# A 1x1 depthwise-separable convolution: halved weight loads with per-slice waits, dummy matmuls ahead of the data, PSUM emptied by ScalarE alone, and last stores split by partitions

## The chip, the cores and the metric

The kernel runs on one core of a Trainium2 chip. The metric is the device time of one execution in microseconds (us). The comparison quantity is the median over several executions. A separate, profiled execution gives the profile; its times are counted from the first instruction of its span.

The core has five engines that run their own instruction queues: TensorE (matmuls, "PE", with its weight loads "PEld"), VectorE ("DVE"), ScalarE ("ACT"), GpSimd ("POOL") and SyncE ("SP", here only a queue of DMA issues). They wait for one another through semaphores. ScalarE can issue DMAs too. SBUF is the working memory of 128 partitions; PSUM holds the results of matmuls in 8 banks.

## The reference

The input `x` is an image of 384 x 384 pixels with 384 channels, in bf16. The depthwise kernel `dw` has size 1 x 1, so the depthwise step multiplies each channel by one number, and the pointwise step is a matrix product with `pw` (384 x 384):

```
B, H, W, C = x.shape                       # 1, 384, 384, 384
out = xp * dw[0, 0][None, None, None, :]   # k = 1: no padding
return jnp.einsum('bhwc,cd->bhwd', out, pw)
```

So out[n, d] = sum over c of x[n, c] * dw[c] * pw[c, d], for 147,456 pixels n. Both `x` and the output are 113.2 MB.

## The kernel before, in words

**Tiling.** The pixels are cut into 288 supertiles of 512 pixels. Supertiles are grouped into 42 chunks, which are the units of loads and stores: 1, 1, 2, 4, then 34 chunks of 8, then 4, 2, 1, 1. A chunk of 8 supertiles is 3 MB. There are three input buffers `X` and three output buffers `O`, used in turn by chunk (t mod 3), two buffers `T` of transposed data and two sets `PS` of four PSUM banks, used in turn by supertile (s = even or odd).

**Weights.** `pw_r` receives four copies of `pw`, one for each group q of 32 partitions; it has six slices b with two halves r (or par) each. Each copy is one DMA (`load_pw`, L89), two of them issued by ScalarE and two by SP. `dwsel` gets the numbers `dw` from a small load `dwt` by four VectorE copies (L186). VectorE makes six of the twelve scaled slices `w_r` (L197) and ScalarE the other six (L199). The first of each waits until all four loads have landed (`s_pw` at 64).

**A supertile.** VectorE transposes it from `X` to `T` in two instructions, h = 0 and 1 (L174), each for three slices b; pairs of bf16 numbers are moved as one 32-bit word. TensorE then runs 6 x 2 x 4 = 48 matmuls (L134): slice b, half par, row group q. The four q use different 32-row strips of the array and different PSUM banks, so they run side by side; the 12 steps over (b, par) accumulate. The matmuls stand in a hardware loop of 144 iterations, two supertiles in each. Ahead of the loop TensorE waits for all twelve slices `w_r`. Within it, it waits for each half of `T`, and at the first step for the PSUM banks to be empty: for ScalarE (`s_a`) at q = 0 and for VectorE (`s_d`) at q = 3.

**Emptying PSUM.** When a supertile's matmuls are done, ScalarE copies the banks of q = 0 to 2 to `O` (L215, 128 x 1152 elements), and VectorE the bank of q = 3 (L212, 128 x 384). VectorE's queue alternates: the copy of supertile jj, then the two transposes of supertile jj + 2. A transpose waits until TensorE has read the old content of that half of `T`. At the first supertile of a chunk both wait until the store that used this `O` buffer three chunks ago has landed (`s_o`).

**Loads and stores.** SP issues everything in a fixed order: `load_x(0)`, the weights, `load_x(1)`, `load_x(2)`, and then for each chunk t `load_x(t + 3)` (L95) and `store(t)` (L107). `load_x(t + 3)` waits until chunk t has been transposed, and `store(t)` until chunk t's last copies are done. As the queue is in order, a load behind a waiting store waits too. At the end SP waits for all stores.

Of the kernel before, what the change touches and what calls it, by code (L numbers as in the profile page):

```python
# [7 lines left out]
BF16 = mybir.dt.bfloat16  # L8
F32 = mybir.dt.float32
U32 = mybir.dt.uint32  # L10
COPY = mybir.ActivationFunctionType.Copy
# [3 lines left out]
NO = 3  # L15
# [11 lines left out]
def kernel(  # L27
# [11 lines left out]
    nc = tc.nc  # L39
    P = nc.NUM_PARTITIONS  # L40
    B, H, W, C = x.shape
    assert dw.shape[0] == 1 and dw.shape[1] == 1, "only k=1 depthwise supported"
    D = pw.shape[1]
    N = B * H * W
    assert C == 384 and D == 384 and N % 1024 == 0
    NB = C // 64

    xf = x.rearrange("b h w c -> (b h w) c")
    of = out.rearrange("b h w d -> (b h w) d")

    NS = N // 512
    chunks = _chunks(NS)
    NT = len(chunks)
    s0 = [sum(chunks[:t]) for t in range(NT)]

    consts = ctx.enter_context(tc.tile_pool(name="consts", bufs=1))
# [3 lines left out]
    pw_r = consts.tile([P, NB, 2, D], BF16, name="pw_r")  # L60
    w_r = consts.tile([P, NB, 2, D], BF16, name="w_r")
    dwt = consts.tile([32, NB, 2], BF16, name="dwt")
    dwsel = consts.tile([P, NB * 2], F32, name="dwsel")
    warm = consts.tile([P, 3], F32, name="warm")
    seed = consts.tile([P, 2], F32, name="seed")

    Xs = [bufp.tile([P, 4 * LMAX, C], BF16, name=f"X{i}") for i in range(NX)]
    Ts = [bufp.tile([P, NB, 256], BF16, name=f"T{i}") for i in range(2)]
    Os = [bufp.tile([P, 4 * LMAX * D], BF16, name=f"O{i}") for i in range(NO)]
    PS = [psum.tile([P, 4, 512], F32, name=f"ps{s}") for s in range(2)]  # L70
# [2 lines left out]
    s_t = [[nc.alloc_semaphore(f"s_t{i}{h}") for h in range(2)] for i in range(2)]  # L73
    s_pe = nc.alloc_semaphore("s_pe")
    s_a = [nc.alloc_semaphore(f"s_a{i}") for i in range(2)]
    s_d = [nc.alloc_semaphore(f"s_d{i}") for i in range(2)]
    s_o = [nc.alloc_semaphore(f"s_o{i}") for i in range(NO)]
    s_dw = nc.alloc_semaphore("s_dw")
    s_pw = nc.alloc_semaphore("s_pw")
    s_ds = nc.alloc_semaphore("s_ds")  # L80
    s_wr = nc.alloc_semaphore("s_wr")
    s_seed = nc.alloc_semaphore("s_seed")

    with tc.tile_critical():  # L84
        pw_v = pw.rearrange("(b w r) d -> w b (r d)", w=32, r=2)
        dw_v = dw.rearrange("a e (b w r) -> w (a e b) r", w=32, r=2)

        def load_pw(eng, q):
            eng.dma_start(pw_r[32 * q : 32 * q + 32].rearrange("w b r d -> w b (r d)"), pw_v).then_inc(s_pw, 16)  # L89

        def load_x(t):
            L = chunks[t]
            r = 512 * s0[t]
            src = xf[r : r + 512 * L, :].rearrange("(p s) c -> p (s c)", p=P)
            d = nc.sync.dma_start(Xs[t % NX][:, : 4 * L, :].rearrange("p s c -> p (s c)"), src)  # L95
            if t >= NX:
                je = s0[t - NX] + chunks[t - NX] - 1
                d._wait_ge(s_t[je % 2][1], je // 2 + 1)
            d.then_inc(s_x[t % NX], 16)

        def store(t):
            L = chunks[t]
            r = 512 * s0[t]
            je = s0[t] + L - 1
            nc.sync.wait_ge(s_d[je % 2], je // 2 + 2)
            dst = of[r : r + 512 * L, :].rearrange("(q p j) d -> p q (j d)", q=4, p=P)
            d = nc.sync.dma_start(dst, Os[t % NO][:, : 4 * L * D].rearrange("p (q e) -> p q e", q=4))  # L107
            d._wait_ge(s_a[je % 2], je // 2 + 2)
            d.then_inc(s_o[t % NO], 16)


        nc.scalar.dma_start(dwt[:], dw_v).then_inc(s_dw, 16)
        load_x(0)
        load_pw(nc.scalar, 2)
        load_pw(nc.sync, 0)
        load_pw(nc.scalar, 3)
        load_pw(nc.sync, 1)
        for t in range(1, NX):
            load_x(t)
        for t in range(NT):  # L120
            if t + NX < NT:
                load_x(t + NX)
            store(t)
        for o in range(NO):
            nc.sync.wait_ge(s_o[o], 16 * len(range(o, NT, NO)))


        def supertile(s, rv):
            for b in range(NB):
                for par in range(2):  # L130
                    for q in range(4):
                        if par == 0 and q == 0 and b in (0, 3):
                            nc.tensor.wait_ge(s_t[s][b // 3], rv)
                        mm = nc.tensor.matmul(  # L134
                            PS[s][:, q, :D],
                            lhsT=Ts[s][32 * q : 32 * q + 32, b, par::2],
                            rhs=w_r[32 * q : 32 * q + 32, b, par, :],
                            start=(b == 0 and par == 0),
                            stop=(b == NB - 1 and par == 1),
                            tile_position=(32 * q, 0),  # L140
                        )
                        if b == 0 and par == 0 and q == 0:
                            mm._wait_ge(s_a[s], rv)
                        elif b == 0 and par == 0 and q == 3:
                            mm._wait_ge(s_d[s], rv)
                        if b in (2, 5) and par == 1 and q == 3:
                            mm.then_inc(s_pe)

        nc.tensor.wait_ge(s_wr, 2 * NB)
        with nc.tensor.Fori(0, NS // 2, 1) as it:  # L150
            rv = nc.tensor.to_reg(it + 1)
            for s in range(2):
                supertile(s, rv)


        for s in range(2):
            nc.vector.memset(seed[:, s : s + 1], 0.0).then_inc(s_d[s])  # L157
        nc.gpsimd.memset(warm[:], 0.0).then_inc(s_seed)  # L158
        for s in range(2):
            c = nc.scalar.copy(warm[:, s + 1 : s + 2], warm[:, 0:1])  # L160
            if s == 0:
                c._wait_ge(s_seed, 1)
            c.then_inc(s_a[s])

        def transposes(t, j):
            jj = s0[t] + j
            L = chunks[t]
            s = jj % 2
            Xw = Xs[t % NX][:].bitcast(U32)[:, : 4 * L, :].rearrange("p (k l) c -> p k l c", l=L)
            Tw = Ts[s][:].bitcast(U32).rearrange("p b (i k) -> p b k i", k=4)  # L170
            for h in range(2):
                if h == 0 and j == 0:
                    nc.vector.wait_ge(s_x[t % NX], 16 * (t // NX + 1))  # L173
                ins = nc.vector.transpose(  # L174
                    out=Tw[:, 3 * h : 3 * h + 3],
                    in_=Xw[:, :, j, 96 * h : 96 * h + 96].rearrange("p k (b w) -> p b k w", w=32),
                )
                if jj >= 2:
                    ins._wait_ge(s_pe, 2 * (jj - 2) + h + 1)
                ins.then_inc(s_t[s][h])  # L180

        order = [(t, j) for t in range(NT) for j in range(chunks[t])]

        nc.vector.wait_ge(s_dw, 16)
        for q in range(4):
            nc.vector.tensor_copy(  # L186
                dwsel[32 * q : 32 * q + 32, :], dwt[:].rearrange("w b r -> w (b r)")
            ).then_inc(s_ds)
        transposes(*order[0])
        for b in range(NB):  # L190
            for r in range(2):
                eng = nc.vector if r == 0 else nc.scalar
                if b == 0:
                    eng.wait_ge(s_pw, 64)  # L194
                sc = dwsel[:, 2 * b + r : 2 * b + r + 1]
                if r == 0:
                    i = nc.vector.tensor_scalar_mul(w_r[:, b, r, :], pw_r[:, b, r, :], sc)  # L197
                else:
                    i = nc.scalar.activation(w_r[:, b, r, :], pw_r[:, b, r, :], COPY, scale=sc)  # L199
                if b == 0:  # L200
                    i._wait_ge(s_ds, 4)
                i.then_inc(s_wr)
        transposes(*order[1])

        for jj, (t, j) in enumerate(order):
            L = chunks[t]
            s = jj % 2
            Ov = Os[t % NO][:, : 4 * L * D].rearrange("p (q j d) -> p q j d", q=4, d=D)
            if j == 0 and t >= NO:
                nc.vector.wait_ge(s_o[t % NO], 16 * (t // NO))  # L210
                nc.scalar.wait_ge(s_o[t % NO], 16 * (t // NO))  # L211
            e = nc.vector.tensor_copy(Ov[:, 3, j, :], PS[s][:, 3, :D])  # L212
            e._wait_ge(s_pe, 2 * jj + 2)
            e.then_inc(s_d[s])
            a = nc.scalar.copy(Ov[:, 0:3, j, :], PS[s][:, 0:3, :D])  # L215
            a._wait_ge(s_pe, 2 * jj + 2)
            a.then_inc(s_a[s])
            if jj + 2 < NS:
                transposes(*order[jj + 2])


# [28 lines left out]
```

## Time and profile before

| what | value |
|---|---|
| median of 7 executions | 586.64 us (585.72 to 587.04) |
| profiled execution, its own time | 585.4 us |
| profiled execution, span from first to last instruction | 583.6 us |
| mean granted TensorE clock | 0.996 |
| TensorE matmuls busy | 563.5 us (97%), 13,824 instructions |
| VectorE busy | 563.9 us (97%) |
| ScalarE busy | 326.8 us (56%) |
| data moved by the DMA | 227.79 MB, mean 390 GB/s over the span |
| chain that ended last | PE 93%, DMA 5%, ACT 1% |

An engine's busy time is the time in which at least one of its instructions runs, so overlapping matmuls count once. The chain that ended last is followed back from the last instruction, at each step to what released it; what has a large share there sets the time. A group of instructions is one line of the kernel on one engine; "idle before" is the time in which the engine stood still just ahead of such an instruction. Lines such as L134 are line numbers of the kernel above.

### The profile page before, as it was taken

To read this page: it belongs to the slowest core of one execution; us is meant where nothing else is said; L and a number is where in the kernel's file an instruction comes from. 1 tells how busy PE (TensorE), PEld (TensorE's weight loads), DVE (VectorE), ACT (ScalarE), POOL (GpSimd) and SP (SyncE) were. 2 spreads that over 40 slices of the span, in tenths; PEclk is the share of its full clock that TensorE was granted. 3 is DMA by queue.
4 is the path that set the end of the run, shared out by engine and by line. 5 is a ranking of instruction groups with operands and counts; after the bars stand their busy time and mean duration, and the time that the engine had idled before them with its cause. 6 is when DMAs were issued, how large, how long until landed. Compare 5 with 4: busy or idle time off the path is not lost.

```text
span 583.6 us, 29852 instructions
## 1 busy us (share of the span) xinstructions
PE 563.5 (97%) x13824; PEld 412.9 (71%) x13824; DVE 563.9 (97%) x876; ACT 326.8 (56%) x297; POOL 0.3 (0%) x5
## 2 busy tenths in 40 slices
PE   1999999999999999999999999999999999999995
PEld 0667777777777777777777777777777777777773
DVE  3899999999999999999999999999999999999995
ACT  3555555555555555555656565555555555555553
POOL 0000000000000000000000000000000000000000
PEclk9999999999999999999999999999999999999998
DMA  8699999999999999999999999999999999999858
GB/s 295 247 429 421 426 424 425 418 386 403 418 388 400 416 389 390 415 387 417 408 392 415 395 409 418 389 409 402 400 409 400 390 401 419 393 394 419 324 222 312
DMA packets 29277, 227.79 MB, mean 390 GB/s; under 512 B 1616, under 2 KB 5456, under 8 KB 24656
## 3 DMA queue, kind: packets, MB, share of 16 engines
q1 hardware_dynamic: 28640, 227.09, 97.1%
q10 hardware_dynamic: 624, 0.59, 0.4%
q14 instruction: 12, 0.10, 0.0%
q8 instruction: 1, 0.02, 0.0%
HBM read 114.43 MB, written 113.25 MB: 390 GB/s over the span
## 4 chain that ended last, share of the span: by engine, by line
PE 93%; DMA 5%; ACT 1%; SPq 0%; issue 0%; DVE 0%; ACTq 0%; DVEq 0%
PE ps L134 93%; DMA X<-in_x_dram 2%; DMA out_dram<-O 1%; DMA pw_r<-in_pw_dram 1%; ACT O L215 1%; ACT w_r L199 1%; DVE T L174 0%; SPq L89 0%; SPq L107 0%; SPq L95 0%; SPq L245 0%; DVEq L173 0%; ACTq L211 0%; ACTq L194 0%; SPq L84 0%
## 5 line engine op out<-in xcount | busy, mean ns | idle before, releaser
L134 PE MATMUL ps<-w_r,T 32*128 32x384 bf16 x13824 | 563.5, 322 | 13.8 <-ACT w_r L199 13.0
L134 PEld LDWEIGHTS ps<-w_r,T 32*128 32x128 bf16 x13824 | 412.9, 93 | 164.0 <-issue 14.3
L215 ACT CAST O<-ps 128x1152 bf16<-128x1152 f32 x288 | 322.1, 1118 | 244.7 <-PE ps L134 242.9
L174 DVE STREAM_TRANSPOSE T<-X 128x384 uint32<-128x384 uint32 x576 | 449.8, 857 | 1.3 <-DMA X<-in_x_dram 1.2
L212 DVE CAST O<-ps 128x384 bf16<-128x384 f32 x288 | 160.4, 557 | 6.5 <-PE ps L134 4.3
L199 ACT ACTIVATE w_r<-pw_r,dwsel 128x384 bf16<-128x384 bf16 x6 | 3.1, 602 | 5.6 <-DMA pw_r<-in_pw_dram 5.6
L186 DVE CAST dwsel<-dwt 32x12 f32<-32x12 bf16 x4 | 0.7, 164 | 3.7 <-DMA dwt<-in_dw_dram 3.6
L197 DVE TENSOR_SCALAR w_r<-pw_r,dwsel 128x384 bf16<-128x384 bf16 x6 | 1.5, 316 | 2.5 <-DMA pw_r<-in_pw_dram 2.5
L160 ACT ACT_TABLE_LOAD x1 | 1.3, 1283 | 2.3 <-issue 2.3
L157 DVE MEMSET seed<- 128x1 f32 x2 | 0.1, 59 | 1.0 <-SPq L84 1.0
L160 ACT COPY warm<-warm 128x1 f32<-128x1 f32 x2 | 0.3, 188 | 0.0
L234 POOL MEMSET const-bfloat16-1.0<- 128x1 bf16 x1 | 0.1, 101 | 0.0
L234 POOL MEMSET const-uint8-127<- 128x1 uint8 x1 | 0.1, 101 | 0.0
L158 POOL MEMSET warm<- 128x3 f32 x1 | 0.1, 100 | 0.5 <-SPq L84 0.5
L234 POOL MEMSET const-float32-0.0<- 128x1 f32 x1 | 0.1, 98 | 0.2 <-issue 0.2
L234 POOL MEMSET const-float32-1.0<- 128x1 f32 x1 | 0.1, 98 | 0.0
## 6 DMA issues: line engine op xcount, KB each, us to landing
X<-in_x_dram SPq DMA_DIRECT2D x34, 3072.0 KB, 18.0
out_dram<-O SPq DMA_DIRECT2D x34, 3072.0 KB, 23.2
X<-in_x_dram SPq DMA_DIRECT2D x2, 1536.0 KB, 12.5
out_dram<-O SPq DMA_DIRECT2D x2, 1536.0 KB, 13.6
X<-in_x_dram SPq DMA_DIRECT2D x4, 384.0 KB, 5.6
X<-in_x_dram SPq DMA_DIRECT2D x2, 768.0 KB, 10.1
out_dram<-O SPq DMA_DIRECT2D x4, 384.0 KB, 3.8
out_dram<-O SPq DMA_DIRECT2D x2, 768.0 KB, 11.3
```

The source lines that it names most:

```text
L134: mm = nc.tensor.matmul(PS[s][:, q, :D], lhsT=Ts[s][32 * q : 32 * q + 32, b, par::2], rhs=w_r[32 * q : 32 * q + 32, b, par, :], start=(b = ...
L157: nc.vector.memset(seed[:, s : s + 1], 0.0).then_inc(s_d[s])
L158: nc.gpsimd.memset(warm[:], 0.0).then_inc(s_seed)
L160: c = nc.scalar.copy(warm[:, s + 1 : s + 2], warm[:, 0:1])
L174: ins = nc.vector.transpose(out=Tw[:, 3 * h : 3 * h + 3], in_=Xw[:, :, j, 96 * h : 96 * h + 96].rearrange("p k (b w) -> p b k w", w=32),)
L186: nc.vector.tensor_copy(dwsel[32 * q : 32 * q + 32, :], dwt[:].rearrange("w b r -> w (b r)")).then_inc(s_ds)
L197: i = nc.vector.tensor_scalar_mul(w_r[:, b, r, :], pw_r[:, b, r, :], sc)
L199: i = nc.scalar.activation(w_r[:, b, r, :], pw_r[:, b, r, :], COPY, scale=sc)
L212: e = nc.vector.tensor_copy(Ov[:, 3, j, :], PS[s][:, 3, :D])
L215: a = nc.scalar.copy(Ov[:, 0:3, j, :], PS[s][:, 0:3, :D])
L234: nc = _bacc.Bacc("TRN2", target_bir_lowering=False, num_devices=1)
```

## The change

The weights are loaded in eight DMAs in place of four: each copy is cut into slices b = 0 to 2 (h = 0) and b = 3 to 5 (h = 1), with a semaphore for each half. The four copies to `dwsel` move to ScalarE. VectorE makes nine of the slices `w_r` and ScalarE three (b = 0, 2, 4 of r = 1). Ahead of the loop TensorE waits only for the first slice; within the loop, in the even supertile, the q = 0 matmul of each further step waits for its own slice. These waits stay in the loop in all 144 iterations.

Ahead of the first real matmul, TensorE runs 14 matmuls on a tile of zeros, which GpSimd fills.

ScalarE copies all four banks in one instruction (128 x 1536 elements). VectorE copies nothing, except in the last supertile, where ScalarE takes two banks and VectorE the other two. `s_d` is left for that alone, and TensorE and the stores wait for `s_a` only.

The stores of chunks 38, 39 and 40 (4, 2 and 1 supertiles) are split in two DMAs each by partitions: 120 and 8, 104 and 24, 56 and 72. The last store is split by banks: SP issues one half and ScalarE the other.

```diff
--- before.py
+++ after.py
@@ -62,7 +62,7 @@
     dwt = consts.tile([32, NB, 2], BF16, name="dwt")
     dwsel = consts.tile([P, NB * 2], F32, name="dwsel")
     warm = consts.tile([P, 3], F32, name="warm")
-    seed = consts.tile([P, 2], F32, name="seed")
+    zero = consts.tile([P, D], BF16, name="zero")
 
     Xs = [bufp.tile([P, 4 * LMAX, C], BF16, name=f"X{i}") for i in range(NX)]
     Ts = [bufp.tile([P, NB, 256], BF16, name=f"T{i}") for i in range(2)]
@@ -73,20 +73,25 @@
     s_t = [[nc.alloc_semaphore(f"s_t{i}{h}") for h in range(2)] for i in range(2)]
     s_pe = nc.alloc_semaphore("s_pe")
     s_a = [nc.alloc_semaphore(f"s_a{i}") for i in range(2)]
-    s_d = [nc.alloc_semaphore(f"s_d{i}") for i in range(2)]
+    s_d = nc.alloc_semaphore("s_d")
     s_o = [nc.alloc_semaphore(f"s_o{i}") for i in range(NO)]
     s_dw = nc.alloc_semaphore("s_dw")
-    s_pw = nc.alloc_semaphore("s_pw")
+    s_pw = [nc.alloc_semaphore(f"s_pw{h}") for h in range(2)]
     s_ds = nc.alloc_semaphore("s_ds")
-    s_wr = nc.alloc_semaphore("s_wr")
+    s_wr = [nc.alloc_semaphore(f"s_wr{e}") for e in range(2)]
     s_seed = nc.alloc_semaphore("s_seed")
+    s_zero = nc.alloc_semaphore("s_zero")
+    s_last = nc.alloc_semaphore("s_last")
 
     with tc.tile_critical():
         pw_v = pw.rearrange("(b w r) d -> w b (r d)", w=32, r=2)
         dw_v = dw.rearrange("a e (b w r) -> w (a e b) r", w=32, r=2)
 
-        def load_pw(eng, q):
-            eng.dma_start(pw_r[32 * q : 32 * q + 32].rearrange("w b r d -> w b (r d)"), pw_v).then_inc(s_pw, 16)
+        def load_pw(eng, q, h):
+            bs = slice(3 * h, 3 * h + 3)
+            eng.dma_start(
+                pw_r[32 * q : 32 * q + 32, bs].rearrange("w b r d -> w b (r d)"), pw_v[:, bs]
+            ).then_inc(s_pw[h], 16)
 
         def load_x(t):
             L = chunks[t]
@@ -98,31 +103,54 @@
                 d._wait_ge(s_t[je % 2][1], je // 2 + 1)
             d.then_inc(s_x[t % NX], 16)
 
+        split = {NT - 4: 120, NT - 3: 104, NT - 2: 56}
+        s_cut = {t: [nc.alloc_semaphore(f"s_cut{t}_{i}") for i in range(2)] for t in split}
+
         def store(t):
             L = chunks[t]
             r = 512 * s0[t]
             je = s0[t] + L - 1
-            nc.sync.wait_ge(s_d[je % 2], je // 2 + 2)
             dst = of[r : r + 512 * L, :].rearrange("(q p j) d -> p q (j d)", q=4, p=P)
-            d = nc.sync.dma_start(dst, Os[t % NO][:, : 4 * L * D].rearrange("p (q e) -> p q e", q=4))
-            d._wait_ge(s_a[je % 2], je // 2 + 2)
-            d.then_inc(s_o[t % NO], 16)
+            src = Os[t % NO][:, : 4 * L * D].rearrange("p (q e) -> p q e", q=4)
+            nc.sync.wait_ge(s_a[je % 2], je // 2 + 2)
+            if t in split:
+                c = split[t]
+                nc.sync.dma_start(dst[:c], src[:c]).then_inc(s_cut[t][0], 16)
+                nc.sync.dma_start(dst[c:], src[c:]).then_inc(s_cut[t][1], 16)
+            else:
+                nc.sync.dma_start(dst, src).then_inc(s_o[t % NO], 16)
 
 
         nc.scalar.dma_start(dwt[:], dw_v).then_inc(s_dw, 16)
         load_x(0)
-        load_pw(nc.scalar, 2)
-        load_pw(nc.sync, 0)
-        load_pw(nc.scalar, 3)
-        load_pw(nc.sync, 1)
+        for h in range(2):
+            for q in range(2):
+                load_pw(nc.scalar, 2 + q, h)
+                load_pw(nc.sync, q, h)
         for t in range(1, NX):
             load_x(t)
-        for t in range(NT):
+        for t in range(NT - 1):
             if t + NX < NT:
                 load_x(t + NX)
             store(t)
+        o_last = Os[(NT - 1) % NO][:, : 4 * D].rearrange("p (q e) -> p q e", q=4)
+        of_last = of[N - 512 :, :].rearrange("(q p) d -> p q d", p=P)
+        nc.sync.dma_start(of_last[:, 2:4], o_last[:, 2:4])._wait_ge(s_d, 1).then_inc(
+            s_last, 16
+        )
         for o in range(NO):
-            nc.sync.wait_ge(s_o[o], 16 * len(range(o, NT, NO)))
+            nc.sync.wait_ge(s_o[o], 16 * len([t for t in range(o, NT - 1, NO) if t not in split]))
+        for t in split:
+            for c in s_cut[t]:
+                nc.sync.wait_ge(c, 16)
+        nc.sync.wait_ge(s_last, 32)
+
+
+        wr_eng = {(b, r): int(r == 1 and b % 2 == 0) for b in range(NB) for r in range(2)}
+        wr_done, made = {}, [0, 0]
+        for k, e in wr_eng.items():
+            made[e] += 1
+            wr_done[k] = (s_wr[e], made[e])
 
 
         def supertile(s, rv):
@@ -141,21 +169,31 @@
                         )
                         if b == 0 and par == 0 and q == 0:
                             mm._wait_ge(s_a[s], rv)
-                        elif b == 0 and par == 0 and q == 3:
-                            mm._wait_ge(s_d[s], rv)
+                        elif s == 0 and q == 0:
+                            mm._wait_ge(*wr_done[b, par])
                         if b in (2, 5) and par == 1 and q == 3:
                             mm.then_inc(s_pe)
 
-        nc.tensor.wait_ge(s_wr, 2 * NB)
+
+        nc.tensor.wait_ge(s_zero, 1)
+        for i in range(14):
+            nc.tensor.matmul(
+                PS[1][:, i % 4, :D],
+                lhsT=zero[32 * (i % 4) : 32 * (i % 4) + 32, 0:P],
+                rhs=zero[32 * (i % 4) : 32 * (i % 4) + 32, :],
+                start=True,
+                stop=True,
+                tile_position=(32 * (i % 4), 0),
+            )
+        nc.tensor.wait_ge(*wr_done[0, 0])
         with nc.tensor.Fori(0, NS // 2, 1) as it:
             rv = nc.tensor.to_reg(it + 1)
             for s in range(2):
                 supertile(s, rv)
 
 
-        for s in range(2):
-            nc.vector.memset(seed[:, s : s + 1], 0.0).then_inc(s_d[s])
         nc.gpsimd.memset(warm[:], 0.0).then_inc(s_seed)
+        nc.gpsimd.memset(zero[:].bitcast(U32), 0).then_inc(s_zero)
         for s in range(2):
             c = nc.scalar.copy(warm[:, s + 1 : s + 2], warm[:, 0:1])
             if s == 0:
@@ -181,25 +219,24 @@
 
         order = [(t, j) for t in range(NT) for j in range(chunks[t])]
 
-        nc.vector.wait_ge(s_dw, 16)
+        nc.scalar.wait_ge(s_dw, 16)
         for q in range(4):
-            nc.vector.tensor_copy(
-                dwsel[32 * q : 32 * q + 32, :], dwt[:].rearrange("w b r -> w (b r)")
-            ).then_inc(s_ds)
+            nc.scalar.copy(dwsel[32 * q : 32 * q + 32, :], dwt[:].rearrange("w b r -> w (b r)")).then_inc(s_ds)
         transposes(*order[0])
-        for b in range(NB):
-            for r in range(2):
-                eng = nc.vector if r == 0 else nc.scalar
-                if b == 0:
-                    eng.wait_ge(s_pw, 64)
-                sc = dwsel[:, 2 * b + r : 2 * b + r + 1]
-                if r == 0:
-                    i = nc.vector.tensor_scalar_mul(w_r[:, b, r, :], pw_r[:, b, r, :], sc)
-                else:
-                    i = nc.scalar.activation(w_r[:, b, r, :], pw_r[:, b, r, :], COPY, scale=sc)
-                if b == 0:
-                    i._wait_ge(s_ds, 4)
-                i.then_inc(s_wr)
+        first = {}
+        for (b, r), e in wr_eng.items():
+            eng = (nc.vector, nc.scalar)[e]
+            if (e, b // 3) not in first:
+                eng.wait_ge(s_pw[b // 3], 64)
+            sc = dwsel[:, 2 * b + r : 2 * b + r + 1]
+            if e == 0:
+                i = nc.vector.tensor_scalar_mul(w_r[:, b, r, :], pw_r[:, b, r, :], sc)
+            else:
+                i = nc.scalar.activation(w_r[:, b, r, :], pw_r[:, b, r, :], COPY, scale=sc)
+            if (e, b // 3) not in first and b == 0:
+                i._wait_ge(s_ds, 4)
+            first[e, b // 3] = True
+            i.then_inc(s_wr[e])
         transposes(*order[1])
 
         for jj, (t, j) in enumerate(order):
@@ -207,16 +244,26 @@
             s = jj % 2
             Ov = Os[t % NO][:, : 4 * L * D].rearrange("p (q j d) -> p q j d", q=4, d=D)
             if j == 0 and t >= NO:
-                nc.vector.wait_ge(s_o[t % NO], 16 * (t // NO))
-                nc.scalar.wait_ge(s_o[t % NO], 16 * (t // NO))
-            e = nc.vector.tensor_copy(Ov[:, 3, j, :], PS[s][:, 3, :D])
-            e._wait_ge(s_pe, 2 * jj + 2)
-            e.then_inc(s_d[s])
-            a = nc.scalar.copy(Ov[:, 0:3, j, :], PS[s][:, 0:3, :D])
+                if t - NO in split:
+                    for c in s_cut[t - NO]:
+                        nc.scalar.wait_ge(c, 16)
+                        nc.vector.wait_ge(c, 16)
+                else:
+                    nc.scalar.wait_ge(s_o[t % NO], 16 * (t // NO))
+            nq = 4
+            if jj + 1 == NS:
+                nq = 2
+                e = nc.vector.tensor_copy(Ov[:, nq:4, j, :], PS[s][:, nq:4, :D])
+                e._wait_ge(s_pe, 2 * jj + 2)
+                e.then_inc(s_d)
+            a = nc.scalar.copy(Ov[:, 0:nq, j, :], PS[s][:, 0:nq, :D])
             a._wait_ge(s_pe, 2 * jj + 2)
             a.then_inc(s_a[s])
             if jj + 2 < NS:
                 transposes(*order[jj + 2])
+        nc.scalar.dma_start(of_last[:, 0:2], o_last[:, 0:2])._wait_ge(s_a[(NS - 1) % 2], (NS - 1) // 2 + 2).then_inc(
+            s_last, 16
+        )
 
 
 # ---- launch: one core; inputs and outputs as the reference has them ----
```

## The prediction

> **What bounds the kernel now.** I read the profiled execution first as a chain of waits in order of time, since the question is which wait ends last at each stage.
>
> ```profile
> 1.88 7.54 DMA pw_r<-in_pw_dram
> ...
> 9.51 3.15 ACT w_r L199 x6
> ...
> 12.98 3.73 PE ps L134 x42
> ...
> 16.73 1.13 ACT O L215
> ...
> 17.88 0.40 SPq L107
> ...
> 18.32 11.73 DMA X<-in_x_dram
> ...
> 31.15 538.40 PE ps L134 x13248
> ...
> 570.72 7.55 DMA out_dram<-O
> ...
> 578.35 1.12 ACT O L215
> ```
>
> Columns: start, duration, what. There are three stages. In the head, TensorE starts at 12.98, after all four weight loads (landed 9.42) and six ScalarE multiplies. From 31.15 TensorE runs without a break: 538.40 us / 276 supertiles = 1.951 us each. In the tail, the last ScalarE copy waits for a store.
>
> The stretches show that two resources have little to spare:
>
> ```profile
> core 0: us, PE busy (x) PEld busy (x) DVE busy (x) ACT busy (x) POOL busy (x), PEclk, DMA share, GB/s
> 12.98:16.20 3.22, 3.22 (x44) 1.84 (x48) 0.00 (x0) 0.00 (x0) 0.00 (x0) 1.00 0.55 229
> 200.00:300.00 100.00, 100.00 (x2470) 73.76 (x2464) 100.00 (x155) 57.24 (x52) 0.00 (x0) 1.00 1.01 404
> 556.00:562.00 6.00, 6.00 (x156) 4.44 (x148) 6.00 (x11) 3.51 (x4) 0.00 (x0) 1.00 0.20 54
> 572.00:576.00 4.00, 4.00 (x104) 2.86 (x100) 3.87 (x7) 2.34 (x3) 0.00 (x0) 1.00 0.99 398
> ```
>
> The first 3.22 us hold 44 matmuls (13.7 per us), the middle 24.7 per us: the first supertile runs at half rate although the clock column reads 1.00. Singly, four matmuls start every 0.320 us until 16.2 and every 0.1625 us later; 12 x 0.1625 = 1.950, so the middle has no bubble in it. The DMA rests at 556 to 562 and is full from about 563 until 581.
>
> ```profile
> L134 PE MATMUL ps<-w_r,T 32*128 32x384 bf16 x13824 | 563.5, 322 | 13.8 <-ACT w_r L199 13.0
> L215 ACT CAST O<-ps 128x1152 bf16<-128x1152 f32 x288 | 322.1, 1118 | 244.7 <-PE ps L134 242.9
> L174 DVE STREAM_TRANSPOSE T<-X 128x384 uint32<-128x384 uint32 x576 | 449.8, 857 | 1.3 <-DMA X<-in_x_dram 1.2
> L212 DVE CAST O<-ps 128x384 bf16<-128x384 f32 x288 | 160.4, 557 | 6.5 <-PE ps L134 4.3
> ```
>
> ScalarE has 0.83 us of idle time per supertile. VectorE is busy throughout, but it sets nothing: TensorE's idle time has a single wait of 0.8 us for a transpose, at 30 us.
>
> [...]full rate comes 3.24 us after the first matmul. [...]
>
> **Part 1, the head.** Before, the completion count of the weights shows a first pair of loads landed by 6.97 and all by 9.42. The order of bytes is x chunk 0, then weights. The first halves are as many bytes as that pair, on the same two queues behind the same chunk, so I take 6.97 for them (bounds 6.4 and 7.6) and 9.42 for the second halves, since the total is unchanged. Issues go from 4 to 8, about 0.45 us each: SP reaches x chunks 1 and 2 about 0.9 us later (2.37 to 3.3) and ScalarE ends issuing at 3.2, its table load and warm copies at 4.8. The four dwsel copies move to ScalarE (4 x 0.19 = 0.76, priced by its small copies at 188 ns) and end at 5.6: hidden by the weight load, which lands 1.4 us later. VectorE, free of them, transposes supertile 0 at 5.0 to 6.5, also hidden.
>
> Then: landing 6.97 + 0.10 (as 9.42 to 9.52) + 0.32 (one VectorE multiply) + 0.33 (loop set-up, as 12.65 to 12.98) puts TensorE's start at 7.72, 5.26 us earlier. Three slices at half rate are 6 x 0.32 = 1.92, so it wants slice 3 at 9.64; that is ready at 9.42 + 0.10 + 0.32 + 0.05 = 9.89. Another 6 x 0.32 ends supertile 0 at 11.8. It was 16.71, so 4.9 us are won. VectorE now makes nine slices; its five after 9.52 take 5 x 0.245 = 1.23, and the transpose of supertile 1 (0.87) is ready at 11.7: just hidden. ScalarE's three multiplies fit beside them.
>
> What is late next is chunk 4. Its load is queued on SP behind the store of chunk 0, which waits for the first copy, and that copy is longer by part 2. It took 11.73 us from 18.32; now it starts 4.9 - 0.32 = 4.58 earlier, lands near 25.5, and supertile 8 starts at 31.15 - 4.58 = 26.6. TensorE would be ready at 11.8 + 7 x 1.95 = 25.45, so a stall of about 1.1 us takes the place of the 0.8. Everything later shifts by 4.6 (bounds 3.5, if bytes land later or chunk 4 contends with chunk 3, which lands at 15.74; and 5.6).
>
> **Part 2, dummy matmuls.** Zeroing 192 words on GpSimd isn't in the trace beyond 0.10 us for three elements. [...] In four row groups, 14 take 3.5 x 0.32 = 1.1 us and end near 2.8. A gap of 4.9 us follows, [...]so I count no gain. If the clock were full after all, slice 3 would still wait for 9.42, and supertile 0 would end 0.5 us sooner. I take 0 of 0 to 0.5. A loss is excluded: nothing else uses TensorE or that PSUM buffer then.
>
> **Part 3, ScalarE alone.** From 1118 ns for 1152 elements at 0.833 ns ([...]960 ns) 158 are fixed, so 1536 elements take 1.44 us, 0.32 longer. Handshakes of some 0.07 make 1.51 of 1.95: TensorE waits for nothing (0.4 to spare). VectorE loses 0.48 of its 1.95 us; it was off the path, so that is 0, but transposes end about 1.1 us earlier against TensorE, and loads are issued earlier. The removed memsets are 0.1 us, hidden. Only the store issue behind each copy is 0.32 later; that counts in the head (done) and tail. Every q = 0 matmul of the even supertile gets a wait: 11 x 144 = 1,584, each long satisfied. The four waits per supertile in the kernel before cost nothing visible: 1.951 against 1.950. So I take 0, with 0.3 us as the upper bound (0.2 ns each).
>
> **Part 4, the tail.** Store 37 (8 supertiles) is issued at 562.92 after a DMA pause, and from it the queue never empties: fast engines end store 37 at 572.7, x chunk 41 at 573.6, store 38 at 577.4, 39 at 579.35, 40 at 580.45. One of 16 engines lags, by 0.8 us at store 38. Splitting by 120 and 8 partitions [...](15 and 8 engines), 104 and 24 use 13 and 12, 56 and 72 use 14 and 12. Per-engine load becomes 9, 10 and 10 partitions where it was 8: 3.75 x 9/8 = 4.22, 1.93 x 10/8 = 2.41, 1.07 x 10/8 = 1.34, together 7.97 against 6.75. From 573.6 + 0.32 (late copy) the queue is empty at 581.9, and the last store (1.0) ends at 582.9 where it ended at 582.26. The halved last copy (VectorE 157 + 768 x 1.04 = 0.96 us against 1.12) is hidden: it waits for store 38 till about 578.1 and issues by 579.7, ahead of the queue. So the tail costs +0.6. Lower bound -0.6: if the 16 engines share one rate, the uneven load is free. Upper bound +1.4[...].
>
> **Sum** against this execution: 583.6 - 4.6 + 0.6 = 579.6 of span; with its 1.8 us outside the span, 585.4 becomes 581.4. The seven runs' median is 586.64, 1.24 above this execution. I carry most of that difference, since a run whose clock rises later loses in supertile 1 what the stall before supertile 8 partly absorbs: 582.5.
>
> **Rivals.**
> (a) The tail helps, or the clock is warm: head -5.1, tail -0.6, hence 581.0. For it: one engine lags, so a split has something to avoid. Against it: the tail's 398 GB/s is already what the middle gets, and 4.9 us of idle array.
> (b) The head is held by the DMA: the window 8 to 14 us already moves up to 440 GB/s, and chunk 4 competes with chunk 3 as it didn't before (the DMA rested at 16 to 18). Supertile 8 starts only 2.5 us earlier, hence 584.7. Against it: 11.73 us for 3 MB contains slack.
> (c) The other side: the waits in the loop are exposed. Each stands on a weight load that is pulled ahead of the running matmuls. At 2.5 ns each, 1,584 of them eat the 4.0 us; at 4 ns it is +6.3, hence 589. Against it: weight loads with a wait start 1 to 2 ns behind the previous matmul, like those without.
>
> **Chances.** My forecast 0.47, (a) 0.28, (b) 0.15, (c) 0.07, anything else slower 0.03. Under 0.2% (1.2 us) a measurement can't be told from no change. (a) and my forecast are faster, (b) mostly (0.13): faster 0.88, same 0.03, slower 0.09. The range runs from (a)'s good end (580.3) to (b)'s bad end (585.2).
>
> **What would show it.** Right: first real matmul near 7.7, supertile 1 near 11.8, a stall of about 1 us near 26; ScalarE copies of 1.44 us with 0.5 idle; period still 1.951; last landing 0.6 us later against TensorE's end. Wrong: a period over 1.96, four-matmul spacing of 0.16 us at 8 us, or chunk 4 landing after 27.

## The result, and the profile after

The changed kernel takes 589.13 us (median of 15 executions, 587.22 to 591.48), beside 586.58 us for the kernel before (35 executions). The ratio is 1.0047, with a 95% interval of 1.0038 to 1.0056: 0.5% slower, where 582.5 was forecast. Its profiled execution took 589.35 us, with a span of 587.6.

The chain of waits of the changed kernel, with start, duration and what:

```profile
1.88 5.14 DMA pw_r<-in_pw_dram
...
7.12 0.56 DVE w_r L233 x2
...
7.78 3.82 PE ps L162 x48
...
11.63 1.45 ACT O L259
...
13.54 12.89 DMA X<-in_x_dram
...
27.53 540.09 PE ps L162 x13248
...
569.55 10.82 DMA out_dram<-O
...
580.49 0.96 DVE O L256
```

The head is what the prediction says as far as the first copy: TensorE starts at 7.78 and the copy of supertile 0 at 11.63, where it was 16.73, so 5.1 us are won. At supertile 8 only 3.6 are left (27.53 against 31.15). The last two lines are the tail: the store of chunk 38 takes 10.82 us (7.55 before), and the last copy starts at 580.49, later than before, though TensorE was done earlier.

The groups of instructions of the changed kernel:

```profile
L162 PE MATMUL ps<-w_r,T 32*128 32x384 bf16 x13824 | 565.3, 322 | 7.3 <-DVE w_r L233 5.0 <-DVE T L212 2.3
L212 DVE STREAM_TRANSPOSE T<-X 128x384 uint32<-128x384 uint32 x576 | 503.0, 877 | 66.7 <-DMA X<-in_x_dram 11.4 <-PE ps L162 1.4
...
L259 ACT CAST O<-ps 128x1536 bf16<-128x1536 f32 x288 | 413.8, 1437 | 157.6 <-PE ps L162 152.1 <-DMA out_dram<-O 5.5
```

The four-bank copy takes 1437 ns; 1.44 us was worked out. TensorE's wait for the transpose of supertile 8 has grown from 0.8 to 2.3 us. ScalarE waits 5.5 us for a store.

The stretches of the changed kernel after that wait and in the tail:

```profile
core 0: us, PE busy (x) PEld busy (x) DVE busy (x) ACT busy (x) POOL busy (x), PEclk, DMA share, GB/s
...
28.00:32.00 4.00, 4.00 (x68) 2.57 (x60) 3.01 (x5) 1.08 (x1) 0.00 (x0) 0.57 0.96 412
...
572.00:576.00 4.00, 3.39 (x84) 2.29 (x76) 1.57 (x2) 2.42 (x2) 0.00 (x0) 1.00 0.94 256
576.00:580.00 4.00, 0.00 (x0) 0.00 (x0) 0.00 (x0) 0.00 (x0) 0.00 (x0) 0.73 0.76 188
```

From 28 to 32 the granted clock is 0.57: the record of clock changes has it at half from 28.27 for 3.41 us, in which four matmuls start every 0.320 us (every 0.162 us from 33 on), and that costs 1.7 us. From 572 to 580 the DMA moves 256 and then 188 GB/s at shares of 0.94 and 0.76; before, it moved 398 and 391. From 576 to 580 in the kernel before, with the same columns:

```profile
576.00:580.00 4.00, 1.33 (x36) 0.72 (x24) 0.69 (x2) 1.66 (x2) 0.00 (x0) 0.93 1.05 391
```

**Where the time went**, from the two profiled executions. TensorE's last matmul ends at 575.39 instead of 577.33, 1.94 us earlier: 5.10 won by the first copy, less 2.70 between the copies of supertiles 7 and 8 (5.65 where it was 2.95), less 0.47 in supertile 9. Of the 3.17 lost, 1.7 are the halved clock and 1.5 the longer wait. From the last matmul to the end of the span it is 12.17 us instead of 6.29, so 5.88 are lost. Together +3.9, the difference of the spans (587.6 and 583.6). The copies of supertiles 7 and 8 in the changed kernel, which started at 30.38 and 33.33 before:

```profile
25.28 1.44 ACT L259 CAST O<-ps 128x1536 bf16<-128x1536 f32 x1 [0.51 <-PE ps L162]
30.92 1.44 ACT L259 CAST O<-ps 128x1536 bf16<-128x1536 f32 x1 [4.21 <-PE ps L162]
```

### The profile page after: what moved, and what is told of

Read it like the earlier page. It is cut to its first block, busy times and chain, and to the rows that moved or that the text cites. A ratio compares the mean times of both kernels' runs of the same rounds, so it can differ in the third digit from the quotient of the medians.

```text
span 587.6 us, 29668 instructions
## 1 busy us (share of the span) xinstructions
PE 566.8 (96%) x13838; PEld 424.9 (72%) x13838; DVE 506.1 (86%) x586; ACT 417.8 (71%) x298; POOL 0.5 (0%) x6
## 4 chain that ended last, share of the span: by engine, by line
PE 93%; DMA 5%; ACT 0%; DVE 0%; SPq 0%; issue 0%; DVEq 0%
PE ps L162 93%; DMA X<-in_x_dram 2%; DMA out_dram<-O 2%; DMA pw_r<-in_pw_dram 1%; ACT O L259 0%; DVE O L256 0%; DVE T L212 0%; DVE w_r L233 0%; SPq L92 0%; SPq L118 0%; SPq L121 0%; SPq L100 0%; DVEq L250 0%; SPq L292 0%; DVEq L211 0%
## 5 line engine op out<-in xcount | busy, mean ns | idle before, releaser
L212 DVE STREAM_TRANSPOSE T<-X 128x384 uint32<-128x384 uint32 x576 | 503.0, 877 | 66.7 <-DMA X<-in_x_dram 11.4
L162 PEld LDWEIGHTS ps<-w_r,T 32*128 32x128 bf16 x13824 | 424.5, 93 | 148.5 <-issue 8.6
L259 ACT CAST O<-ps 128x1536 bf16<-128x1536 f32 x288 | 413.8, 1437 | 157.6 <-PE ps L162 152.1
L235 ACT ACTIVATE w_r<-pw_r,dwsel 128x384 bf16<-128x384 bf16 x3 | 1.7, 610 | 2.5 <-DMA pw_r<-in_pw_dram 2.5
L180 PE MATMUL ps<-zero 32*128 32x384 bf16 x14 | 1.5, 513 | 1.3 <-POOL zero L196 1.3
```

The costliest lines, as they stand in the source:

```text
L162: mm = nc.tensor.matmul(PS[s][:, q, :D], lhsT=Ts[s][32 * q : 32 * q + 32, b, par::2], rhs=w_r[32 * q : 32 * q + 32, b, par, :], start=(b = ...
L180: nc.tensor.matmul(PS[1][:, i % 4, :D], lhsT=zero[32 * (i % 4) : 32 * (i % 4) + 32, 0:P], rhs=zero[32 * (i % 4) : 32 * (i % 4) + 32, :], s ...
L212: ins = nc.vector.transpose(out=Tw[:, 3 * h : 3 * h + 3], in_=Xw[:, :, j, 96 * h : 96 * h + 96].rearrange("p k (b w) -> p b k w", w=32),)
L259: a = nc.scalar.copy(Ov[:, 0:nq, j, :], PS[s][:, 0:nq, :D])
```

## The experiments

All times are medians, each against runs of the kernel before on the same chip. The runs e9 to e11 were on another chip than e1 to e8, so between these two groups the ratios are what to compare. The last column is from the profiled execution.

| run | time, us | ratio to before (95%) | last matmul to end, us |
|---|---|---|---|
| changed kernel | 589.13 | 1.0047 (1.0038 to 1.0056) | 12.17 |
| e1 one DMA per store | 582.79 | 0.9933 (0.9912 to 0.9954) | 6.00 |
| e2 stores split by banks | 583.19 | 0.9945 (0.9929 to 0.9962) | 6.06 |
| e3 cut at partition 64 | 586.46 | 0.9991 (0.9981 to 1.0001) | 9.99 |
| e4 before, with the split | 592.76 | 1.0102 (1.0085 to 1.0118) | 13.18 |
| e11 even and odd partitions | 583.43 | 0.9947 (0.9920 to 0.9974) | 6.05 |
| e5 chunk 4 loaded first | 587.97 | 1.0019 (1.0010 to 1.0027) | 5.98 |
| e6 the same, no dummies | 588.05 | 1.0021 (1.0011 to 1.0031) | 5.99 |
| e7 before, with ScalarE alone | 586.86 | 1.0002 (0.9994 to 1.0011) | 6.38 |
| e8 small first chunks | 579.36 | 0.9874 (0.9857 to 0.9890) | 5.98 |
| e9 the same, 64 dummies | 579.78 | 0.9896 (0.9879 to 0.9912) | 5.98 |
| e10 as e8, no dummies | 580.01 | 0.9887 (0.9871 to 0.9904) | 6.00 |

### The tail: what in the split is slow

Three theories. P: pieces cut by partitions make the engines meet at the same partitions of SBUF. L, the prediction's: only the number of partitions per engine counts. N: the second issue per store costs, in SP's queue. The changed kernel's queue of SP gives N some colour:

```profile
573.00 0.31 SPq L118 DMA_DIRECT2D out_dram<-O  x1
573.36 2.25 SPq L119 DMA_DIRECT2D out_dram<-O  x1
575.65 3.19 SPq L118 DMA_DIRECT2D out_dram<-O  x1
578.88 1.35 SPq L119 DMA_DIRECT2D out_dram<-O  x1
```

In the kernel before, each issue of these stores took 0.37 to 0.39 us. Here the first of the four still takes 0.31, the other three 1.35 to 3.19.

**e1** puts one DMA back for each of the three stores (and lets VectorE wait for the store that frees the last `O` buffer).

```diff
-        split = {NT - 4: 120, NT - 3: 104, NT - 2: 56}
+        split = {}
```

> The changed kernel with the stores of chunks 38 to 40 undone to one DMA each. Theory P (a store cut by partitions makes the 16 engines meet at the same partitions, so their packets get slower): TensorE's end stays near 575.4, and from there to the end of the span takes about 6.6 us as in the kernel before (6.3) where the changed kernel took 12.2; some 5 us faster than the changed kernel, near 584. Theory L, the prediction's (only the uneven number of partitions per engine counts): 1.2 us faster, near 588. Theory N (a second issue per store is what costs, through SP's queue): as P.

Measured: 582.79, 6.3 us under the changed kernel, and 6.00 us of tail. The split alone turns the change's gain into a loss, and L, which gives 1.2, falls as the whole cause.

**e4** adds the split, and nothing else, to the kernel before: the same `split`, `s_cut` and waits as in the change. (SP's wait for ScalarE becomes an instruction of its own for every store, as in the change.)

> The kernel before with nothing changed but the cut of the stores of chunks 38 to 40 at partitions 120, 104 and 56. P and N: 4 to 6 us slower than before, 591 to 593. L: 1.2 us slower, 587.8.

Measured: 592.76, 6.1 us slower than the 586.67 beside it, with a tail of 13.18 us. So the price belongs to the split, whatever the head and the copies are.

**e2** keeps two DMAs for each store, but cuts the free dimension.

```diff
-                nc.sync.dma_start(dst[:c], src[:c]).then_inc(s_cut[t][0], 16)
-                nc.sync.dma_start(dst[c:], src[c:]).then_inc(s_cut[t][1], 16)
+                nc.sync.dma_start(dst[:, :2], src[:, :2]).then_inc(s_cut[t][0], 16)
+                nc.sync.dma_start(dst[:, 2:], src[:, 2:]).then_inc(s_cut[t][1], 16)
```

> The changed kernel, but each of the three stores is split in two DMAs by PSUM bank (q 0 to 1, q 2 to 3), so all 128 partitions are in each. P: within 0.7 us of the kernel with one store each, packets of 3072 bytes keep near 121 ns. N: as slow as the changed kernel, near 589, with issues of 2 to 3 us on SP. L: as with one store each.

Measured: 583.19 and a tail of 6.06 us, within the runs' scatter of e1. Two issues per store cost nothing, and N falls. None of these six issues took over 0.56 us, so the long issues go with the slow pieces and not with the number of issues. That they follow from engines that are behind is argued: in e5, below, an issue of a load took 4.37 us behind 3 MB, with nothing split.

**e3** cuts at 64, so that both halves hold as many partitions.

```diff
-        split = {NT - 4: 120, NT - 3: 104, NT - 2: 56}
+        split = {NT - 4: 64, NT - 3: 64, NT - 2: 64}
```

> The changed kernel with all three cuts at partition 64, so that [...]16 engines take part in each half, 4 partitions each. L: the load is even, so as fast as with one store each, near 584. P: each half reaches only half of the partitions, so it is as slow as the changed kernel or slower (589 to 593), with packets of 3072 bytes well over 121 ns. N: near 589.

Measured: 586.46, 3.7 us slower than e1, less than P had said (589 to 593), and a tail of 9.99 us in the profiled execution. That execution was the slowest of the thirteen (590.48), since TensorE had waited 4.1 us for chunk 4 in it, long ahead of the tail. The 16 engines' share of busy time was 0.99 from 574 to 578 and from 578 to 582 (0.76 in the changed kernel from 576 to 580), so the load is even, and yet it is slow. SP's queue in e3, for chunks 39 and 40:

```profile
576.32 0.59 SPq L118 DMA_DIRECT2D out_dram<-O  x1
576.96 2.48 SPq L119 DMA_DIRECT2D out_dram<-O  x1
579.49 2.34 SPq L118 DMA_DIRECT2D out_dram<-O  x1
581.87 1.18 SPq L119 DMA_DIRECT2D out_dram<-O  x1
```

**e11** takes 64 partitions in each half too, but every second one.

```diff
-                nc.sync.dma_start(dst[:c], src[:c]).then_inc(s_cut[t][0], 16)
-                nc.sync.dma_start(dst[c:], src[c:]).then_inc(s_cut[t][1], 16)
+                nc.sync.dma_start(dst[0::2], src[0::2]).then_inc(s_cut[t][0], 16)
+                nc.sync.dma_start(dst[1::2], src[1::2]).then_inc(s_cut[t][1], 16)
```

> The changed kernel with the three stores split in even and odd partitions, so that 16 engines take part in each half with 4 partitions each, as with the cut at 64, but each half reaches all of the partition range. P: packets of 3072 bytes at 121 ns, and the time of the kernel with one store each, 583 to 584. Rival (any DMA of fewer than 128 partitions is slow): as the cut at 64, 586 to 588.

Measured: 583.43 and a tail of 6.05 us. The same four issues in e11:

```profile
571.83 0.60 SPq L117 DMA_DIRECT2D out_dram<-O  x1
572.48 0.64 SPq L118 DMA_DIRECT2D out_dram<-O  x1
573.78 0.60 SPq L117 DMA_DIRECT2D out_dram<-O  x1
574.42 0.63 SPq L118 DMA_DIRECT2D out_dram<-O  x1
```

In e3 and e11 the numbers of DMAs and of partitions in each are the same, and the 16 engines have no rest in either (a DMA share of 1.02 and 1.07 in e11 from 570 to 574 and from 574 to 578). Only which partitions a piece holds differs, and with them the addresses in DRAM. This decides: none of these four issues is above 0.64 us in e11, against 2.48 in e3. The DRAM side alone is unlikely: the pieces of e2 are unbroken blocks of DRAM, and they were fast.

The packet records show the same. A packet of 3072 bytes, the size of chunk 38, takes 121 ns (median) in the stores of the kernel before, of e1, e2 and e11. Of the 512 packets of that store, some 320 took over 200 ns in e3 (median 233 from 576 to 578), and some 240 in the changed kernel (median 450 for the last 14, from 578 to 580). The others mostly kept 121.

In e3 the slow packets took 1.9 times as long (233 ns beside 121), in the changed kernel up to 3.7 times (450). What delays them isn't shown: theory P's meeting of engines at the same partitions remains the author's guess. The packets of chunks 39 and 40 (1536 and 768 bytes), split in the same way, kept their medians of 65 and 36 ns in e3 and in the changed kernel, and the runs don't show why. What they do show is that the large packets of a piece of neighbouring partitions are slow, and that those of pieces spread over all partitions aren't.

Long packets are not the whole price. Over 121, 65 and 36 ns, the packets of these sizes in the tail of the changed kernel took 40 us more in all, which is 2.5 us for each of 16 engines. The tail lost 5.9. In e3, with its even load, it is 3.2 of 4.0. In the changed kernel the engines also drift apart: the landings of the second piece of chunk 39, one per engine, lie between 577.95 and 583.85, where those of any piece in e3 lie within 1.7 us, and the DMA's share falls to 0.76 (e3 from 578 to 582: 0.99). So some engines rest while others are behind, and the uneven load of theory L has a part in the price, too. How large it is was not measured apart.

### The head: what chunk 4 takes back

**e5** moves the load of chunk 4 ahead of the store of chunk 0 on SP, on top of e1.

```diff
-            if t + NX < NT:
+            if t + NX < NT and t != 1:
                 load_x(t + NX)
+            if t == 0:
+                load_x(NX + 1)
             store(t)
```

> The changed kernel with one DMA per store of chunks 38 to 40, and the load of chunk 4 issued ahead of the store of chunk 0 on SP. Theory C (the head's gain is cut twice by chunk 4: TensorE waits 2 us for it, and after that wait its clock falls to half for [...]3.41 us, another 1.7 us): chunk 4 lands 1 to 1.5 us earlier, the wait falls to about 1 us, the clock stays up, and the time is 2 to 3 us under the kernel with one store each (582.8), near 580. Rival D (the DMA's rate alone decides when chunk 4 is there): it lands as late, the order gains under 0.5 us, and the clock falls as before.

Measured: 587.97, which is slower than e1 by 5.2 us. Neither theory had it. ScalarE's timeline in e5:

```profile
15.88 1.44 ACT L263 CAST O<-ps 128x1536 bf16<-128x1536 f32 x1 [0.51 <-PE ps L164]
17.83 1.44 ACT L263 CAST O<-ps 128x1536 bf16<-128x1536 f32 x1 [0.51 <-PE ps L164]
26.28 2.78 ACT L263 CAST O<-ps 128x1536 bf16<-128x1536 f32 x2 [7.01 <-DMA out_dram<-O]
```

The store of chunk 0 now stands behind 3 MB of load, lands at 26.2, and frees the output buffer that chunk 3 needs: ScalarE waits 7.01 us, TensorE behind it, and the clock falls for 6.83 us. The order on SP that was to be mended protects the output buffers. So this run doesn't test C against D.

**e8** does, by making chunk 4 smaller, on top of e1.

```diff
-    head, tail = [1, 1, 2, 4], [4, 2, 1, 1]
+    head, tail = [1, 1, 2, 4, 4, 4], [4, 2, 1, 1]
```

> The changed kernel with one DMA per store, and with chunks 1, 1, 2, 4, 4, 4 at the head in place of 1, 1, 2, 4, so that chunk 4 is 1.5 MB. C: it lands near 20, TensorE never waits and never loses its clock after the first supertile; 580 minus the last 1 us of wait, so near 579, and less spread between runs. D: the DMA falls behind one chunk later and the wait only moves; 582 and up.

Measured: 579.36 (579.09 to 580.07), 1.3% faster than before, and the fastest of all runs. The chain of waits of e8, its first and last parts:

```profile
7.86 555.69 PE ps L162 x13067
...
565.03 7.01 DMA out_dram<-O
...
572.13 0.96 DVE O L258
```

From 7.86 the chain stays on TensorE to the end of the middle; no wait for `X` is left on it. The clock rises once, at 11.17, and holds until 574.4. TensorE's last matmul ends at 571.32, 4.0 us before that of e1 (575.32): 2 us of waiting and 1.7 us of half clock were what chunk 4 had taken. C holds. Chunk 4 landed at 22.14, later than C's 20, but in time.

### The dummy matmuls

**e6** leaves the 14 dummies out of e5, **e10** leaves them out of e8, and **e9** makes them 64 in e8. The diff is that of e9; in e6 and e10 the loop and the wait for `s_zero` ahead of it are gone.

```diff
-        for i in range(14):
+        for i in range(64):
```

> As the run with chunk 4 loaded first, with the 14 dummy matmuls left out. My step: they end near 2.8 us, 5 us ahead of the data, and gain nothing: within 0.5 us of that run, full clock about 3.4 us after the first real matmul in both. Rival: they bring the clock up earlier, so without them supertile 0 and 1 take 1 us or more longer.

> The kernel with small first chunks and one DMA per store, without any dummy matmuls. My step (14 of them gain nothing): within 0.4 us of 579.4. Rival (they bring the clock up earlier): 1 us or more slower.

> The kernel with small first chunks and one DMA per store (579.4), with 64 dummy matmuls in place of 14. If the clock rises [...]and stays up over the gap to the data (they should end near 5.6, 2.3 us ahead of it), supertile 0 runs at 0.16 us per four matmuls and ends near 10.8, but supertile 1 still waits for its transpose near 11.4: 0.2 to 0.5 us faster. If the clock falls again in the gap: no difference.

e6 stands at 588.05 beside 587.97: no difference, though in a kernel with a large stall. e10 stands at 580.01 (579.21 to 580.22) beside 579.36 (579.09 to 580.07): four executions each, whose ranges overlap, so a gain of some 0.6 us is neither shown nor excluded. The clock rose between 2.86 (e1) and 5.40 us (e2) after the first real matmul in the runs with 14 dummies, and between 3.24 (the kernel before) and 6.05 us (e10) in those without: a spread that the dummies don't order. The last section sets changes of the clock beside TensorE's busy share just ahead of them.

With 64 dummies the clock was up at 5.57 and stayed so over the gap of 1.62 us ahead of the first real matmul. The stretch from the first real matmul on, of e9:

```profile
7.78:11.20 3.42, 2.44 (x48) 1.12 (x48) 2.19 (x8) 1.19 (x3) 0.00 (x0) 1.00 1.06 380
```

and of e10:

```profile
7.70:11.20 3.50, 3.50 (x44) 1.62 (x48) 2.29 (x9) 1.06 (x2) 0.00 (x0) 1.00 1.07 399
```

TensorE does its 48 matmuls in 2.44 us of work and waits the rest, where at half clock it is busy throughout. It gained 0.56 us in supertile 0 and lost it again: 0.59 for the transpose of supertile 1 (2.62 us between the first two copies, 2.03 in e8) and 0.35 for chunk 3 at supertile 4. In time, 579.78 beside 579.36, and by ratio 0.9896 beside 0.9874, so no gain.

### ScalarE alone

**e7** is the kernel before with the four-bank copy alone.

```diff
-            e = nc.vector.tensor_copy(Ov[:, 3, j, :], PS[s][:, 3, :D])
-            e._wait_ge(s_pe, 2 * jj + 2)
-            e.then_inc(s_d[s])
-            a = nc.scalar.copy(Ov[:, 0:3, j, :], PS[s][:, 0:3, :D])
+            a = nc.scalar.copy(Ov[:, 0:4, j, :], PS[s][:, 0:4, :D])
```

> The kernel before with ScalarE alone emptying PSUM, four banks in one copy, and nothing else. My step: the period stays 1.950, the copy takes 1.44 us, and 0.3 us are lost at the head and 0.3 at the tail: 586.6 to 587.3. Rival: a copy that spans four banks holds TensorE, and the period grows by 5 ns or more: 588 and up.

Measured: 586.86 beside 586.73, ratio 1.0002 (0.9994 to 1.0011). The group line of e7:

```profile
L208 ACT CAST O<-ps 128x1536 bf16<-128x1536 f32 x288 | 414.2, 1438 | 153.6 <-PE ps L133 152.2 <-DMA out_dram<-O 1.4
```

The copy is 0.32 us longer, the period unchanged, and VectorE's relief is worth nothing, as reckoned. The 0.833 ns an element that the prediction reckoned with comes out of the two copies: (1437 - 1118) / 384 = 0.831. VectorE's 1.04 does, too: its copies of 768 and 384 elements took 958 ns (changed kernel) and 557 (the kernel before), and (958 - 557) / 384 = 1.044.

## Why the prediction was wrong, by its steps

**The head up to supertile 0: right.** First halves of the weights at 7.02 (6.97 forecast), TensorE at 7.78 (7.72), second halves at 9.21 (9.42), supertile 0 done at 11.6 (11.8).

**The head, chunk 4: the right mechanism, mis-sized.** "It took 11.73 us from 18.32" was carried over as it stood. It took 12.89 from 13.54; chunk 3 was still on the DMA until 15.2, and the pause that the DMA of the kernel before had at 16 to 18 us was gone. This was rival (b)'s argument; that it is the cause is argued from the stretches, not shown apart. The wait was 2.3 us instead of 1.1. It brought a term that the prediction had put at nothing: the clock at half for 3.41 us, another 1.7. The prediction counted no gain from the dummies because of the gap behind them, and didn't ask what a gap does to the clock in the stall that it had itself forecast. A stall of 1.1 us had cost no clock in the kernel before: it stood for 1.14 us between two matmul starts at 30 us, and its clock stayed up until 579.41. e8 shows the two together to be worth 3.4 us.

**Dummies: right to count nothing**, within what the runs can tell; they ended at 2.75 (2.8 forecast), behind 0.26 us of zeroing on GpSimd. The reason was another than the gap behind them. The 14 never brought the clock up, which rose at 10.75 us (e1) or later in every run that has them; 64 did, and that clock outlasted a gap of 1.6 us.

**ScalarE alone: right**, by e7.

**Waits in the loop, rival (c): refuted.** From the copy at 33.34 to that at 567.64 are 274 supertiles, at 1.950 each.

**The tail: the step that made the forecast fail.** The step "Per-engine load becomes 9, 10 and 10 partitions where it was 8" gave +0.6, and +1.4 as its upper bound; measured are +5.9. The engines' numbers were right: the completions that land after each issue count 15 and 8, 13 and 12, 14 and 12. Whether the one that lags is among them, they don't show. The rate of a single engine was taken as given, and it isn't: with the same load per engine, e3 lost 4.0 us of tail and e11 nothing, so it depends on which partitions a piece holds. The low bound (-0.6, "if the 16 engines share one rate") and the high one (the engine that lags gets the uneven load, too) both varied the load and never the packet's duration. None of the forecast's three signs of being wrong looked at the tail, and none of them showed: the period was 1.950, the first supertile ran at half rate, and chunk 4 landed at 26.43, ahead of 27.

The two steps make up the miss: 579.6 us of span were forecast and 587.6 measured, 8.0 more. Of these, 2.7 are the head (4.6 forecast, 1.9 left at the last matmul) and 5.3 the tail (+0.6 forecast, +5.9 measured). That e1, the change without its split, took 582.79, close to the 582.5 of the forecast, is in part luck: the span of its profiled execution, 581.3, is 2.3 above the 579.0 that the sum gives without the tail's term, and the 1.1 us that the forecast had added for the median hide some of that.

## What to carry to other kernels

A store that is split should let each piece reach over the whole range of partitions: split the free dimension, or take every second partition. Here a split into blocks of neighbouring partitions cost 3.7 to 6.3 us on some 2.7 MB. Loads were not tried. When the start of a kernel is moved forward, ask of the first large transfer whether it was waiting for its issue or for the bytes ahead of it, and price a TensorE stall with its clock, too. Here a chunk 4 of half the size mended both.

## What the runs showed of the hardware that was not expected

- Packets of 3072 bytes of a store took 121 ns (median) when each piece spanned all partitions (the kernel before, e1, e2, e11). In blocks of 64 (e3) some 320 of 512 took over 200 ns, most of them near 233, and with the splits of the change some 240, up to 450 (median of the last 14).
- An issue of a store on SP took 0.37 to 0.39 us in the tail of the kernel before and 0.60 to 0.73 in e11, and three of the four shown took 1.35 to 3.19 us behind the slow pieces of the change.
- Within each trace, all changes of the granted clock lie a whole number of 3.413 us apart: in the changed kernel 5, 1 and 160 times (up at 11.21, down at 28.27, up at 31.69, down at 577.82), in the kernel before 165 times (up at 16.22, down at 579.41). TensorE's busy share was read in successive stretches of 3.413 us, with a change at the edge of one of them. The clock fell after shares of 33% (changed kernel), 40% (e1), 6% (e3) and 10% (e5), and stayed up after 47% (e11), 51% (e9) and 72% (e2). It rose after 84% (e1), 95% (the kernel before) and 100% (changed kernel), and not after 77% (e10) or 58% (e2). These shares come from one execution of each run, and what decides between them isn't shown.
- The length of a pause alone doesn't decide. Between two matmul starts e11 paused 2.44 us and kept its clock (0.999 granted in the mean over its span); its pause lay in two of these stretches, busy 90% and 47%. The pause of e1, 2.38 us, lay within one, and the clock fell (0.60 from 28 to 32). So of two waits for chunk 4 of nearly the same length, one cost 1.7 us of clock and the other nothing.
